# Backward of a gated MLP and a long convolution: transforms with channels as the moving operand, one hand-placed buffer, and transposes moved into DMA

## Chip, cores, metric

One NeuronCore of a Trainium2 chip. The time is the device time of one launch in microseconds (us), the median of several launches. Some launches fall into a slower state, with a lower granted TensorE clock; all runs quoted are in the fast state, and the granted clock of their profiled launches is 0.95 to 0.99.

## The reference

Forward and backward of one block; S = 2048 positions, D = 512 channels, F = 1376, all in bfloat16. Cut to what matters:

```python
def _A_ref(q, k, v, shift_k, ssm_k, ssm_D):         # long convolution by FFT over 2*S points
    k_shift = sum_t k_pad[:, t:t+S, :] * shift_k[:, 3-t]
    kv = k_shift * v
    y = irfft(rfft(kv, 2*S) * rfft(ssm_k, 2*S))[:S] + kv * ssm_D
    return q * y
def _B_ref(x, w_gate, w_up, w_down):                # gated MLP
    return ((x @ w_gate) * (x @ w_up)) @ w_down
xn  = layernorm(A_q)
out = A_q + _A_ref(xn, ...) + _B_ref(xn, ...)
# outputs: out, and the gradients of A_q, A_k, A_v, shift_k, ssm_k, ssm_D, w_gate, w_up, w_down
```

The gradients need three forward transforms (of the filter, of `kv`, of `xn*grad_out`) and three inverse ones, all as matmuls with sine tables, and the MLP's intermediates (`h`, `dg`, `du`) in two layouts: with F on the partitions for the down projections, with positions on the partitions for the weight gradients.

## The kernel before, in the parts that matter

Three stages: the MLP by chunks of 256 positions, whose intermediates go to DRAM as `HDD`; then the transforms, by blocks of 128 channels, interleaved with the down projections (`YB`); then the weight gradients with the finish.

```python
def f_B(key):                                  # second step of a forward transform: 64 matmuls of 128 columns a call, 768 in all
    ...
    for k0 in range(0, 16, 4):
        pb = psF.tile([128, 4, 2, 128], F32, name="pb", tag="psf")
        for ki in range(4):
            nc.tensor.matmul(pb[:, ki, 0, :], lhsT=E[:, k1, 0, :], rhs=Ar, start=True, stop=False)
            nc.tensor.matmul(pb[:, ki, 0, :], lhsT=E[:, k1, 2, :], rhs=Ai, start=False, stop=True)
            ...                                # two more for the imaginary part
        evac_act(Xh[:, 2 * k0: 2 * (k0 + 4), :], pb[:]...)
def i_B(ikey):                                 # inverse transform: the same, then a transposing DMA from SBUF to SBUF
    ...
    nc.sync.dma_start_transpose(out=Ct[:]..., in_=C_sb[:]...)
def nat_from(hb, fw, nat_ap):                  # weight gradients: HDD blocks transposed on TensorE, evicted by ACT
    pt = psF.tile([128, NJ, 128], BF, name="ptw", tag="psf")
    for j in range(NJ):
        nc.tensor.transpose(pt[:, j, :fw], hb[:fw, j * 128:(j + 1) * 128], ident[:fw, :fw])
    evac_act(nat_ap, pt[:, :, :fw])
```

## Time and profile before

| | before |
|---|---|
| time, median (range, n) | 706.23 us (702.38 to 709.43, 15) |
| first stage: MLP and preparation | 0 to 190 us |
| second stage: transforms, down projections | 190 to 480 us |
| hole: TensorE waits for the first `HDD` read | 480 to 496 us |
| third stage: weight gradients, finish | 496 to 707 us |
| TensorE, VectorE, ScalarE busy | 84%, 55%, 56% |

The stages were cut where the first and last instructions of a tile name stand (`pgu`, `pdx`, `ptw`). The prediction below shows the lines. Read a row of the stretches as: length, then the busy time of each engine with its count, then granted clock, share of the DMA engines' time and their rate. An engine is the bound of a stretch only if its busy time nearly fills the length.

### The profile page before, as it was taken

What the parts mean: (1) busy time and instruction counts of PE and PEld (TensorE: products, weight loads), DVE (VectorE), ACT (ScalarE), POOL (GpSimd) and SP (SyncE); (2) the same over time, 40 slices, a digit from 0 to 9 for tenths busy, and PEclk for the clock granted to TensorE, in tenths of its full rate; (3) what the DMA queues carried; (4) which work ended last, traced back from release to release, by engine and by line L of the source; (5) the groups of instructions that cost most, each with busy time, mean ns of one, the idle gap of its engine ahead of it and who ended that gap; (6) DMA issues with size and microseconds to landing.
All of it is one profiled execution on the core that took longest, in us unless ns stands there. A gap on an engine that the chain in (4) does not pass through costs nothing.

```text
span 706.9 us, 12877 instructions
## 1 busy us (share of the span) xinstructions
PE 591.1 (84%) x5194; PEld 407.2 (58%) x5252; DVE 389.5 (55%) x1016; ACT 395.1 (56%) x563; POOL 8.9 (1%) x21
## 2 busy tenths in 40 slices
PE   0889999999779989988889999871998698797992
PEld 0677877888555656665567665441554454463551
DVE  5898965673431536545555456220585608773652
ACT  2669976865573656653467643230665565374542
POOL 3001000000000000000000000000000000000000
PEclk9999999999899999999999999985999799998997
DMA  8648589754395586966968577779999998998433
GB/s 261 215 160 287 198 239 287 272 198 174 143 349 160 166 228 145 229 153 134 260 132 226 123 214 173 169 168 302 329 296 268 273 253 284 299 298 248 130 125 104
DMA packets 205947, 153.28 MB, mean 217 GB/s; under 512 B 120832, under 2 KB 194624, under 8 KB 203840
## 3 DMA queue, kind: packets, MB, share of 16 engines
q1 hardware_dynamic: 202752, 148.10, 73.7%
q10 hardware_dynamic: 3136, 4.36, 1.9%
q8 instruction: 41, 0.67, 0.4%
q14 instruction: 18, 0.15, 0.1%
HBM read 82.68 MB, written 57.19 MB: 198 GB/s over the span
## 4 chain that ended last, share of the span: by engine, by line
PE 40%; DMA 31%; DVE 10%; ACT 10%; issue 4%; SPq 2%; POOL 0%; POOLq 0%; ACTq 0%; DVEq 0%
DMA Ct<-C_sb 13%; PE pg L730 6%; DMA hb<-HDD 3%; PE pgu L472 3%; DMA nat_in<-in_A_k_dram 3%; PE pgu L474 3%; PE pdh L476 3%; DMA bd_j<-BD 3%; ACT C_sb L574 3%; PE pyc L249 2%; PE pb L551 2%; PE ptw L681 2%; PE pdx L557 2%; DMA BD<-bd 2%; PE pdx L556 2%
## 5 line engine op out<-in xcount | busy, mean ns | idle before, releaser
L730 PE MATMUL pg<-nat,xn_tm 128*128 128x512 bf16 (+1 forms) x374 | 80.1, 366 | 0.8 <-issue 0.2
L574 ACT COPY nat<-ptw 128x2048 bf16<-128x2048 bf16 (+1 forms) x33 | 59.1, 1833 | 31.0 <-PE ptw L681 30.9
L574 ACT CAST Xh<-pb 128x1024 bf16<-128x1024 f32 x48 | 47.2, 1013 | 51.3 <-PE pb L617 50.2
L478 ACT CAST gud<-pgu 128x512 bf16<-128x512 f32 (+1 forms) x88 | 51.9, 590 | 32.7 <-ACT gud L479 16.8
L557 PE MATMUL pdx<-WuT_sb,hd_y 128*128 128x512 bf16 (+1 forms) x173 | 66.1, 382 | 0.4
L556 PE MATMUL pdx<-WgT_sb,hd_y 128*128 128x512 bf16 (+1 forms) x164 | 62.7, 382 | 0.1
L681 PE MATMUL ptw<-ident,hb 128*128 128x128 bf16 (+1 forms) x528 | 40.0, 238 | 26.3 <-DMA hb<-HDD 20.6
L472 PE MATMUL pgu<-xnT_all,Wg_sb 128*128 128x256 bf16 (+1 forms) x352 | 56.0, 278 | 4.3 <-ACT gud L478 4.2
L730 PEld LDWEIGHTS <-xn_tm 128*128 128x128 bf16 x384 | 37.7, 101 | 35.4 <-issue 4.0
L476 PE MATMUL pdh<-goT_all,WdT_sb 128*128 128x256 bf16 (+1 forms) x352 | 55.3, 276 | 0.0
L574 ACT CAST C_sb<-pb 128x512 bf16<-128x512 f32 x96 | 49.8, 591 | 9.4 <-PE pb L644 7.8
L681 PEld LDWEIGHTS <-hb 128*128 128x128 bf16 (+1 forms) x528 | 36.1, 108 | 32.2 <-issue 23.4
L474 PE MATMUL pgu<-xnT_all,Wu_sb 128*128 128x256 bf16 (+1 forms) x352 | 54.6, 276 | 0.0
L574 ACT CAST A_sb<-pa 128x1024 bf16<-128x1024 f32 x48 | 45.4, 1044 | 0.2 <-PE pa L600 0.2
L614 PE MATMUL pb<-A_sb,E 128*128 128x128 bf16 x192 | 42.0, 219 | 4.0 <-ACT A_sb L574 2.5
L797 DVE SCALAR_TENSOR_TENSOR acc<-dks,kvk 128x512 bf16<-128x512 bf16 x64 | 43.8, 685 | 0.6
L551 PE MATMUL pb<-Wd_sb,hd_y 128*128 128x512 bf16 (+1 forms) x159 | 43.7, 379 | 0.4 <-issue 0.2
L641 PE MATMUL pb<-Yh,ET 128*128 128x128 bf16 x192 | 41.9, 218 | 1.7 <-ACT C_sb L574 1.0
L480 DVE TENSOR_TENSOR hdd<-gud 128x256 bf16<-128x256 bf16 (+1 forms) x88 | 25.2, 286 | 31.9 <-ACT gud L478 24.6
L617 PE MATMUL pb<-A_sb,E 128*128 128x128 bf16 x192 | 42.0, 219 | 0.0
L644 PE MATMUL pb<-Yh,ET 128*128 128x128 bf16 x192 | 42.0, 219 | 0.0
L616 PE MATMUL pb<-A_sb,E 128*128 128x128 bf16 x192 | 42.0, 219 | 0.0
(171 smaller groups left out, 1245.2 us busy)
## 6 DMA issues: line engine op xcount, KB each, us to landing
HDD<-hdd SPq DMA_DIRECT2D x8, 2112.0 KB, 8.8
hd_y<-HDD SPq DMA_DIRECT2D x8, 2112.0 KB, 9.8
hb<-HDD SPq DMA_DIRECT2D x30, 512.0 KB, 6.7
BD<-bd SPq DMA_DIRECT2D x16, 512.0 KB, 4.0
bd_j<-BD SPq DMA_DIRECT2D x8, 1024.0 KB, 8.6
CTS<-kv SPq DMA_DIRECT2D x4, 1024.0 KB, 5.1
FS<-kd SPq DMA_DIRECT2D x8, 512.0 KB, 5.4
x_cm<-FS SPq DMA_DIRECT2D x8, 512.0 KB, 5.2
```

The costliest lines, as they stand in the source:

```text
L472: nc.tensor.matmul(pgu[:fw, 0, :], lhsT=Wg_sb[:, c, f0:f0 + fw], rhs=xnT_all[:, c, css], start=(c == 0), stop=(c == NCB - 1))
L474: nc.tensor.matmul(pgu[:fw, 1, :], lhsT=Wu_sb[:, c, f0:f0 + fw], rhs=xnT_all[:, c, css], start=(c == 0), stop=(c == NCB - 1))
L476: nc.tensor.matmul(pdh[:fw, :], lhsT=WdT_sb[:, c, f0:f0 + fw], rhs=goT_all[:, c, css], start=(c == 0), stop=(c == NCB - 1))
L478: nc.scalar.copy(gud[:fw, 0:2, :], pgu[:fw])
L551: nc.tensor.matmul(pb[:], lhsT=hd[:fw, 0, fb, ss], rhs=Wd_sb[:fw, fb, :], start=False, stop=(fb == NFB - 1))
L556: nc.tensor.matmul(pdx[:], lhsT=hd[:fw, 1, fb, ss], rhs=WgT_sb[:fw, fb, :], start=(fb == 0), stop=False)
L557: nc.tensor.matmul(pdx[:], lhsT=hd[:fw, 2, fb, ss], rhs=WuT_sb[:fw, fb, :], start=False, stop=(fb == NFB - 1))
L574: nc.scalar.copy(o, i)
L614: nc.tensor.matmul(pb[:, ki, 0, :], lhsT=E[:, k1, 0, :], rhs=Ar, start=True, stop=False)
L681: nc.tensor.transpose(pt[:, j, :fw], hb[:fw, j * 128:(j + 1) * 128], ident[:fw, :fw])
L730: nc.tensor.matmul(pw[:, :R], lhsT=xn_tm[:, j, rows(c)], rhs=nat[:, j, :R], start=(j == 0), stop=(j == NJ - 1))
L797: nc.vector.scalar_tensor_tensor(acc6[:], dks[:, 0:QS], 1.0, kT6[:, 3 - j:3 - j + QS], op0=ALU.mult, op1=ALU.mult, accum_out=dp[:, j:j + 1])
```

## The change

It is a rewrite of the same three stages, meant to make TensorE's work wider and the transfers larger. The sequence is cut as s = 16p + r, so that plain loads and stores are mostly rows of 2 KB and more; the transforms mix over the partitions, with all 512 channels as the moving operand; their intermediates go through DRAM (`AX`, `CX`). Half-array matmuls (64 columns or 64 rows of weights) stand in pairs. The transposes of `HDD` leave TensorE for transposing DMAs. Everything in SBUF lies in one hand-placed buffer, so all its tiles have the name `big` in the profile. The diff cut to its core:

```diff
-    pb = psF.tile([128, 4, 2, 128], F32, name="pb", tag="psf")     # 1536 matmuls of 128 columns in all
-        nc.tensor.matmul(pb[:, ki, 0, :], lhsT=E[:, k1, 0, :], rhs=Ar, ...)
+    def s_B(i, t):                                                 # 192 of 512 columns on 128x64 of the array
+        px = psF.tile([128, 2, D], F32, name="pX", tag="psf")
+        for cp in range(2):
+            for j in range(2):
+                MM(px[64 * j:64 * j + 64, cp, :], lhsT=E[:, 2 * i + j, cp, :], rhs=a[:, j, t, :], start=True, stop=True)
+        ACOPY(X[:, t, :, :], px[:])
+    def s_Bi(i, pr):                                               # 192 of 512 columns on 64x128 of the array
+        for c in range(2):
+            for j in range(2):
+                q = slice(64 * j, 64 * j + 64)
+                MM(pc[:, j, :], lhsT=ET[q, i, c, :], rhs=Y[q, c, :], start=(c == 0), stop=(c == 1))
+        ACOPY(C[:, :, pr, :], pc[:])
-    nc.sync.dma_start_transpose(out=Ct[:]..., in_=C_sb[:]...)      # 12 of 1 MB, SBUF to SBUF
-    nc.tensor.transpose(pt[:, j, :fw], hb[:fw, ...], ident[...])   # 528 on TensorE
+    ldT(out=dst[:, ch, 0:nf, :]..., in_=HDD[ch, :, t, fb0:fb0 + nf, :]...)   # 72 transposing DMAs from DRAM
...
+    while not SG.done:          # second stage: one transform group, then five matmuls of the down projections
+        SG(1)
+        Y(5)
+    while not (WG.done and CG.done):   # third stage: twelve gradient matmuls, then one step of the finish
+        WG(12)
+        CG(1)
```

## The prediction

> **What bounds the kernel now.** I read the page's totals first, then the busy time by stretch, cut at the first and last start of the tiles `pgu`, `pdx`, `ptw`, then the chain, then the forms.
>
> ```profile
> PE 591.1 (84%) x5194; PEld 407.2 (58%) x5252; DVE 389.5 (55%) x1016; ACT 395.1 (56%) x563; POOL 8.9 (1%) x21
> DMA packets 205947, 153.28 MB, mean 217 GB/s; under 512 B 120832, under 2 KB 194624, under 8 KB 203840
> ...
> PE 40%; DMA 31%; DVE 10%; ACT 10%; issue 4%; SPq 2%; POOL 0%; POOLq 0%; ACTq 0%; DVEq 0%
> ```
>
> ```profile
> 28.00:55.00 27.00, 24.05 (x266) 20.14 (x264) 24.09 (x89) 19.61 (x37) 2.58 (x2) 1.00 0.48 151
> 55.00:190.00 135.00, 128.13 (x1163) 107.56 (x1165) 89.83 (x292) 98.54 (x183) 0.10 (x1) 0.97 0.67 228
> 190.00:480.00 290.00, 255.66 (x2434) 169.23 (x2467) 136.22 (x197) 154.81 (x216) 0.00 (x0) 0.98 0.76 191
> 480.00:496.00 16.00, 3.24 (x31) 3.15 (x32) 0.00 (x0) 1.34 (x1) 0.00 (x0) 0.50 1.11 304
> 496.00:690.00 194.00, 169.26 (x1218) 98.93 (x1235) 116.20 (x349) 108.66 (x113) 0.00 (x0) 0.95 0.87 255
> ```
>
> The columns after the length are PE, PEld, DVE, ACT, POOL busy, then granted clock, DMA share and GB/s. There are three stages: A, the gated MLP and the preparation (to 190 us), bound by PE; B, the transforms and the down projections (190 to 480), PE too, with gaps; a hole of 16 us; C, weight gradients and finish (to 707), where PE is at 87% and DMA at 87% (300 GB/s at a share of 1.00 in 500:550). The chain has only 40% in PE and 31% in DMA, so the loss is in waits between the two.
>
> ```profile
> 100.06 0.60 PE L472 MATMUL pgu<-xnT_all,Wg_sb 128*128 128x256 bf16 x4
> 100.50 0.60 PE L474 MATMUL pgu<-xnT_all,Wu_sb 128*128 128x256 bf16 x4
> 258.40 0.38 PE L556 MATMUL pdx<-WgT_sb,hd_y 128*128 128x512 bf16 x1
> 258.61 0.38 PE L557 MATMUL pdx<-WuT_sb,hd_y 128*128 128x512 bf16 x1
> ```
>
> Start to start, not busy time, is the price of a matmul: four of 256 columns in 0.44 us, 109 ns each; 512 columns 215 ns (216 over longer stretches); 128 columns about 56 ns (16 transposes in 0.89 us).
>
> ```profile
> L622 DVE TENSOR_TENSOR Xh<-Xh,Dbc_bf 128x2048 bf16<-128x2048 bf16 x4 | 4.9, 1225 | 18.9 <-ACT Xh L574 18.8
> L198 DVE TENSOR_TENSOR sm_t<-Xh 128x1024 bf16<-128x1024 bf16 x24 | 16.6, 692 | 32.3 <-ACT Xh L574 30.9
> L821 DVE TENSOR_TENSOR m<-xg_j,y_j 128x512 bf16<-128x512 bf16 x16 | 6.7, 420 | 24.4 <-DMA y_j<-YSC 20.3 <-DMA xg_j<-XN 4.2
> L574 ACT CAST Xh<-pb 128x1024 bf16<-128x1024 f32 x48 | 47.2, 1013 | 51.3 <-PE pb L617 50.2
> L478 ACT CAST gud<-pgu 128x512 bf16<-128x512 f32 x80 | 47.2, 591 | 29.5 <-ACT gud L479 15.5 <-PE pgu L474 5.2 <-DVE hdd L482 4.6
> L649 SPq DMA_TRANSPOSE Ct<-C_sb x12: 4728/5396/8076, 254.8 to 466.6; - x12
> 467.00:473.50 6.50, 2.97 (x14) 1.18 (x12) 0.00 (x0) 0.58 (x1) 0.00 (x0) 0.91 0.94 178
> ```
>
> These are my unit prices: a bf16 product of 2048, 1024, 512 elements takes 1.23, 0.69, 0.42 us (a broadcast operand, as in L622, keeps the rate), an eviction of 1024 or 512 takes 1.01 or 0.59 us. A transposing DMA of 1.05 MB holds the queue 5.4 us and, nearly alone in 467.0 to 473.5, fills the DMA engines at only 178 GB/s.
>
> **What the Trainium skill says.** "TensorE: Matmul & The Clock Gate", section "Wait — 56ns, not 53.3ns?", gives 55.6 and 215.7 ns back to back for 128 and 512 columns; the trace agrees (56 and 215). "TensorEngine Tiling (Array Packing)", section "Key Properties", says that tiles run independently but that a change of tiling mode drains the array; no packed pair runs in this trace, so both are open. "DMA: Bandwidth & Descriptors", section "Latency and other measured facts", gives 261 GB/s for a transposing DMA with a non-contiguous middle dimension; the trace shows 178 for one from SBUF, and none from DRAM. The same page, "Rules for kernel authors", asks for large transfers and contiguous last dimensions; here 120832 of 205947 packets are under 512 B.
>
> **The change part by part.** It is a rewrite with the same three stages, on one hand-placed buffer. The sequence is cut as s = 16p + r, so that loads and stores are rows of 2 KB and more; transforms mix over partitions with time outside and channels as the 512-wide moving operand; intermediates AX and CX go through DRAM.
>
> Matmul columns by the built program (both kernels counted): before about 1.31 million, after 1.165 million; matmuls 5252 to about 3085. At the prices above, by stage:
>
> A. Gate, up and down gradient: 1056 x 109 ns = 115 us, unchanged. First transform 96 x 216 = 21, transposes (128 + 64) x 56 = 11. Together 147 us against about 155 of PE busy there before. ACT: 96 evictions of 512 (88 gate/up, 48 mostly 512 wide for the gradient, so about 136) x 0.59 = 79 us, 48 x 1.01 = 49, sine tables 15: 143. DVE: 48 x (0.42 + 0.69) = 53, 80 products or copies of 1024 = 55, eight copies of 2048 = 10, layer norm 20, tables 15: 153. Bytes: loads 13 MB, AX 12.6, HDD 17.3, KS 2.1, weights 4: about 48 MB, 150 us at 320 GB/s. Four resources are level, so none hides the waits of another. The first MLP chunk started at 24.8 us before; I leave it at 24, since weights and two groups of x come first in both. Then chunk 0 at 14, chunks 1 to 6 at 121, chunk 7 at 14, and 12 for stalls: A ends at 185, 5 earlier than now.
>
> B. Down projections 528 x 216 = 114 us, unchanged (16 identity matmuls go). Transforms: 192 + 192 matmuls of 512 columns, 83 us if one at a time, in place of 1536 x 56 + 192 x 109 + 64 x 216 + 128 x about 50 = 127 us. They use half of the array (64 columns, or 64 rows), in pairs; if each pair overlaps it is 42. I take 50 for them and 15 for draining: 180, and 10 for stalls. ACT: 96 x 1.01 + 32 x 0.59 = 116. DVE per round 2 x 1.23 + 2 x 0.69 + 6 x 0.42 = 6.4, sixteen rounds 102. DMA 38 MB, 115 us. So PE bounds B at 190, with 5 for the change of stage: 195 against 290. The twelve transposing DMAs, 13% of the chain, leave it.
>
> C. PE: weight gradients 176 x 216 + 256 x 216 + 128 x 163 (384 columns) = 114; last transform 64 x 216 + 128 x 56 = 21; shift gradient 64 x 216 = 14: 149. The 528 transposes (30 us of PE), the 64 four-tap matmuls and the 33 evictions of 1.83 us go. DVE per chunk of 256 rows: 17 us (20 products of 1024 at 0.69, six accumulating 512s at 0.7 to 0.77, small ones), 139 in all. DMA: CX 12.6 MB, loads 11.5, outputs 14.7, so 39 MB plain at 300 to 340 GB/s, 115 to 130 us; and 17.3 MB of HDD read by 72 transposing DMAs: 97 us at 178 GB/s, 66 at the page's 261. Sum 181 to 227, more than PE. I take 205 for C, and 8 for the last stores, against 227 now (with its hole). The gain of larger rows is largely spent on transposing in the DMA.
>
> Sum: 185 + 195 + 205 + 8 = 593; I say 595 us, 16% less.
>
> **The rivals.** First, transposing from DRAM is much slower than from SBUF, or holds the in-order SP queue, in which the stores of the finish wait for DVE and the next loads stand behind them. At twice the cost C becomes about 300 and the whole 690: no gain. For it: 178 GB/s and 5.4 us of queue per MB even from SBUF. Against it: the page's 261. Second, the pairs overlap and drain cheaply, and the DMA transposes run at 261: B 165, C 180, whole 545. Third, pairs do not overlap and each of 96 groups drains the array twice: B 225 to 230, whole 630. Fourth, A stalls because ACT, in order, waits for AX stores behind HDD stores of 2.1 MB (8.8 us to landing now): 15 to 20 us more.
>
> **Range and chances.** The middle of B is 165 to 225, of C 180 to 240; errors partly cancel, so 550 to 645. To reach 692 the first rival must hold nearly in full. Faster by over 2%: 0.95; within 2%: 0.03; slower: 0.02.
>
> **What would show it.** In the profile after: A ending at 185 with DVE, ACT and PE each above 75%; the last `po`/`px` at about 380, with PE above 90% in B; starts inside a pair of `pX` or `pC` a few ns apart (overlap) or 216 ns apart (none); in C a DMA share near 1 with PE near 75%, and waits of `pw` for HDD transposes. Rates of those transposes in bytes per busy time settle the first rival. The prediction is wrong if C takes over 240 or under 175, if PE waits in B for ACT or DVE, or if the first stage ends after 200.

## The result

| | before | after |
|---|---|---|
| time, median (range, n) | 706.23 us (702.38 to 709.43, 15) | 585.54 us (584.74 to 589.37, 11) |
| first stage, and what was predicted for it | 190 | 180 (185) |
| second stage | 290 | 178 (195) |
| hole and third stage | 227 | 226 (213) |

The ratio is 0.8302, 95% interval 0.8281 to 0.8323. A ratio here is the mean time of one kernel's fast runs over that of the other's of the same rounds, so it is not quite the ratio of the medians quoted. For experiments the ratio is to the kernel before on the same chip; to set one beside the changed kernel I divide by 0.8302. Differences in us are between medians of different chips (the kernel before has medians of 706 to 710 there), so they can be some 3 us off: x2_plain below is 26 us faster by medians and 29 by ratios.

The page of the changed kernel: totals, packets, chain of waits by engine.

```profile
PE 487.1 (83%) x3043; PEld 255.1 (44%) x3085; DVE 360.3 (62%) x707; ACT 327.4 (56%) x405; POOL 7.7 (1%) x20
DMA packets 123486, 146.85 MB, mean 252 GB/s; under 512 B 89719, under 2 KB 95671, under 8 KB 121526
...
PE 51%; DMA 17%; DVE 16%; ACT 5%; SPq 4%; issue 4%; another core or an unknown queue 0%; ACTq 0%; DVEq 0%
```

TensorE lost 104 us of busy time, and its share of the span stayed; that alone does not show that all of it was on the path (the 30 us of transposes that left the third stage gained nothing there). The bytes are nearly the same, in 60% of the packets, and by the packet records 67,584 of these, of 256 bytes, belong to the new transposes. Now the busy time by stretch, cut at the first MLP chunk, the first `po`, the last `px`, and the last gradient matmul:

```profile
0.00:23.70 23.70, 3.52 (x32) 3.34 (x33) 14.34 (x63) 6.58 (x9) 4.00 (x16) 1.00 0.96 298
23.70:179.90 156.20, 148.27 (x1307) 123.47 (x1320) 126.49 (x233) 126.08 (x192) 2.76 (x3) 1.00 0.79 273
179.90:357.70 177.80, 174.00 (x898) 57.22 (x915) 91.45 (x166) 112.70 (x129) 0.95 (x1) 1.00 0.73 249
357.70:411.00 53.30, 45.82 (x228) 20.09 (x231) 25.71 (x53) 21.77 (x21) 0.00 (x0) 0.97 0.90 243
411.00:545.00 134.00, 108.17 (x553) 48.48 (x556) 75.98 (x146) 51.42 (x50) 0.00 (x0) 0.99 1.01 244
545.00:583.40 38.40, 7.29 (x35) 2.49 (x35) 26.29 (x49) 8.89 (x7) 0.00 (x0) 0.61 0.51 190
```

The second stage is now TensorE almost without gaps (174 of 177.8), and it gave 112 of the 121 us, though part of that is transform work that the change moved into the other two stages (counted below). The third stage gained nothing: from 411 to 545 the DMA engines are full at 244 GB/s, and then comes a tail of 38 us in which TensorE works 7 us and VectorE 26. The chain agrees that the bound has moved: TensorE from 40% to 51%, DMA from 31% to 17%, DVE from 10% to 16%.

The timeline of the second stage (start, length, engine, line, operation, count):

```profile
250.22 0.61 PE L508 MATMUL pC<-big 64*128 64x512 bf16 x4
...
251.95 0.62 PE L477 MATMUL pX<-big 128*64 128x512 bf16 x4
252.50 1.04 PE L442 MATMUL po<-big 128*128 128x512 bf16 x4
```

A group of four half-array matmuls starts at 251.95, and the next full-array one at 252.50: 0.55 us. The single records show two starts 4 ns apart, the next two 236 ns later, and about 310 ns where 216 is usual on either side of the group. So a group costs 0.55 + 0.095 = 0.645 us, and each change between whole and halved array about 0.1.

### The profile page after: what moved, and what is told of

Same layout as the page of the kernel before. It is cut to its first block, busy times and chain, and to the rows that moved or that the text cites.

```text
span 583.4 us, 8223 instructions
## 1 busy us (share of the span) xinstructions
PE 487.1 (83%) x3043; PEld 255.1 (44%) x3085; DVE 360.3 (62%) x707; ACT 327.4 (56%) x405; POOL 7.7 (1%) x20
## 4 chain that ended last, share of the span: by engine, by line
PE 51%; DMA 17%; DVE 16%; ACT 5%; SPq 4%; issue 4%; another core or an unknown queue 0%; ACTq 0%; DVEq 0%
PE pg L353 7%; PE px L450 6%; PE px L448 6%; PE po L442 6%; DMA big<-HDD 5%; PE pw L717 5%; PE pw L704 5%; PE pX L477 4%; PE pC L508 4%; DMA big<-CX 4%; PE pd L360 3%; SPq L690 3%; DMA big<-in_A_shift_k_dram 3%; DVE big L381 2%; DVE big L365 2%
## 5 line engine op out<-in xcount | busy, mean ns | idle before, releaser
L717 PE MATMUL pw<-big 128*128 128x512 bf16 (+1 forms) x384 | 86.4, 365 | 20.2 <-DMA big<-HDD 19.8
L353 PE MATMUL pg<-big 128*128 128x256 bf16 (+1 forms) x704 | 88.2, 273 | 0.4
L353 PEld LDWEIGHTS <-big 128*128 128x128 bf16 (+1 forms) x704 | 69.6, 100 | 12.9
L450 PE MATMUL px<-big 128*128 128x512 bf16 (+1 forms) x172 | 65.4, 380 | 0.9 <-issue 0.8
L448 PE MATMUL px<-big 128*128 128x512 bf16 (+1 forms) x169 | 64.3, 381 | 0.5 <-issue 0.5
L478 ACT CAST big<-pX 128x1024 bf16<-128x1024 f32 x48 | 48.4, 1014 | 25.4 <-PE pX L477 18.1
L509 ACT CAST big<-pC 128x1024 bf16<-128x1024 f32 x48 | 48.6, 1012 | 23.4 <-PE pC L508 20.8
L354 ACT CAST big<-pg 128x512 bf16<-128x512 f32 (+1 forms) x88 | 52.2, 605 | 14.2 <-PE pg L353 13.1
L401 ACT CAST big<-pa 128x1024 bf16<-128x1024 f32 x48 | 48.7, 1035 | 9.1 <-remote 3.9
L360 PE MATMUL pd<-big 128*128 128x256 bf16 (+1 forms) x352 | 47.2, 273 | 1.0 <-ACT big L354 0.7
L442 PE MATMUL po<-big 128*128 128x512 bf16 (+1 forms) x169 | 44.1, 381 | 0.8 <-issue 0.6
L704 PE MATMUL pw<-big 128*128 128x512 bf16 (+1 forms) x172 | 41.2, 389 | 0.4 <-issue 0.3
L721 ACT CAST big<-pw 128x512 bf16<-128x512 f32 (+1 forms) x24 | 13.6, 584 | 44.4 <-DMA out_dram<-big 24.5
L360 PEld LDWEIGHTS <-big 128*128 128x128 bf16 (+1 forms) x352 | 34.8, 100 | 8.2 <-issue 0.9
```

The lines of the kernel that those rows point to most:

```text
L353: MM(pg[:fw, j, :], lhsT=W[:, c, fb * 128:fb * 128 + fw], rhs=T[:, 0, c, :], start=(c == 0), stop=(c == 3))
L354: ACOPY(g[:fw, 0:2, i, :], pg[:fw])
L360: MM(pd[:fw, i, :], lhsT=WdT[:, c, fb * 128:fb * 128 + fw], rhs=T[:, 1, c, :], start=(c == 0), stop=(c == 3))
L401: ACOPY(a[:, :, t, :], pa[:])
L442: MM(po[:], lhsT=h[:fw, 0, fb, ss], rhs=wy["d"][:fw, fb, :], start=(fb == 0), stop=(fb == NFB - 1))
L448: MM(px[:], lhsT=h[:fw, 1, fb, ss], rhs=wy["g"][:fw, fb, :], start=(fb == 0), stop=False)
```

## The experiments

Line numbers of experiments can be a few off those of the changed kernel. Twelve kernels ran; each is correct unless said otherwise.

**x1_unpack: break the pairs by order.** Both uses of one half come first, then both of the other.

```diff
-        for cp in range(2):
-            for j in range(2):
+        for j in range(2):
+            for cp in range(2):        # in s_B; the same swap of c and j in s_Bi
```

> The changed kernel with the two inner loops of the transforms' matmuls swapped, so that of each group of four only the middle two neighbours use different halves of the array; same matmuls, same results. Theory 1 (stage B is bound by PE and the overlap of the pairs is what made it 178 us): each of the 96 groups grows from two steps of 216 ns to three, B by 21 us (to 199), the whole from 585 to 606; 41 us if no neighbours overlap at all. Rival (B is bound by evictions, products or transfers, and the overlap is worth nothing): the whole within 4 us of 585.

Measured: 586.89 us (585.25 to 589.32), ratio 0.8284: no change. That looks as if pairing did not matter, but it doesn't show it. The order is swapped in the built program too, yet the single records still come in pairs 6 to 7 ns apart, and in 43 of the 47 complete `pC` groups the second record carries the semaphore update that only the third matmul of the program has. So, by the records, TensorE started the third, on the free half, ahead of the second, which had to wait for its own half. One `pC` group did run in the program's order, with its third weights loaded late; it shows what the others avoided, 0.78 us to the next start in place of 0.55 (that group, then a usual one):

```profile
201.77 0.85 PE L508 MATMUL pC<-big 64*128 64x512 bf16 x4
202.55 0.62 PE L477 MATMUL pX<-big 128*64 128x512 bf16 x4
```

```profile
250.78 0.61 PE L508 MATMUL pC<-big 64*128 64x512 bf16 x4
251.33 0.39 PE L442 MATMUL po<-big 128*128 128x512 bf16 x1
```

The experiment did not take away what it was to take away; x7_half does.

**x7_half: no pairs at all.** Both matmuls of each pair use the same half.

```diff
-                MM(px[64 * j:64 * j + 64, cp, :], lhsT=E[:, 2 * i + j, cp, :], ...)
+                MM(px[0:64, cp, :], lhsT=E[:, 2 * i + j, cp, :], ...)
-        ACOPY(X[:, t, :, :], px[:])
+        ACOPY(X[0:64, t, :, :], px[0:64])      # the other half of X is set to zero once
-                q = slice(64 * j, 64 * j + 64)
+                q = slice(0, 64)
```

> Swapping the order inside the groups changed nothing (first batch), so this run denies the pairing altogether: all four matmuls of a group go to the same half of the array (the first 64 columns, or the first 64 rows); number, columns and mode changes stay. The result is wrong on purpose (out2 to out5 and what hangs on them). Theory 1 (two matmuls in different halves run side by side, whatever their order in the queue): a group becomes 4 x 216 ns + 0.2 us of change = about 1.05 us in place of 0.645, so 96 groups cost 40 us more; the second stage goes from 178 to about 215 us and the whole to 620 to 630 us. Rival (a matmul on half of the array simply takes half the time by itself): no change, 584 to 590 us.

Measured: 626.37 us (623.08 to 628.25), ratio 0.8827, out2 to out6 wrong. Its timeline and its second stage:

```profile
252.14 1.05 PE L479 MATMUL pX<-big 128*64 128x512 bf16 x4
253.12 1.25 PE L442 MATMUL po<-big 128*128 128x512 bf16 x5
```

```profile
180.00:396.00 216.00, 214.44 (x901) 74.85 (x900) 90.86 (x164) 112.80 (x127) 6.12 (x3) 1.00 0.60 204
```

From group to next start it is now 0.98 us in place of 0.55, so 96 groups cost 96 x 0.43 = 41 us more; the stage went from 178 to 216 (the first gradient matmul starts at 398.5 in place of 358.0). That shows the pairs to overlap and to be worth 38 to 41 us. The rival is refuted: a half-array matmul alone takes as long as a whole one.

**x2_plain: what the transposing reads cost.** The 72 DMAs read the same bytes plainly; out7 to out9 wrong.

```diff
-            ldT(out=dst[:, ch, 0:nf, :].rearrange("p f (r q) -> p (f r) q", r=2), in_=HDD[...]...)
+            ld(dst[:, ch, 0:nf, :].rearrange("p f s -> p (f s)"), HDD[...]...)
```

> The changed kernel with the 72 transposing reads of HDD made plain reads of the same bytes into the same places; three weight gradients are wrong on purpose. Theory 2 (stage C is bound by the DMA engines, and transposing costs them far more than the same bytes plain): 17.3 MB fall from about 97 us of the engines to about 54, C from 226 to 190 to 200 us, the whole to 550 to 560. Rival (C is bound by DVE and PE chains and by the in-order queue; transposing is hidden): the whole stays within 6 us of 585.

Measured: 559.38 us (557.01 to 560.85), ratio 0.789: 26 us less than the changed kernel. The issues of these reads in the SP queue, with minimum, median and maximum in ns, in the changed kernel and then in this one:

```profile
L690 SPq DMA_TRANSPOSE big<-HDD  x72: 1229/1276/4311, 331.3 to 534.4; - x72
```

```profile
L690 SPq DMA_DIRECT2D big<-HDD  x72: 319/382/677, 332.8 to 496.2; - x72
```

The stretches of the third stage in this run:

```profile
357.70:411.00 53.30, 47.69 (x239) 20.83 (x237) 25.72 (x53) 21.58 (x21) 0.00 (x0) 0.97 0.87 292
411.00:520.00 109.00, 102.39 (x560) 48.92 (x559) 74.23 (x145) 51.27 (x50) 0.00 (x0) 0.98 0.88 304
520.00:555.20 35.20, 6.48 (x36) 2.34 (x34) 26.95 (x49) 8.89 (x7) 0.00 (x0) 0.60 0.33 122
```

Transposing, the DMA engines are full at 244 GB/s; plain, they move 304 at a share of 0.88, and TensorE (102 of 109) becomes the bound. By the packet records, those of 256 bytes in the changed kernel less those left in this run, the transposes' 17.3 MB took 103 us of all 16 DMA engines (168 GB/s), and the same bytes plain some 53. The queue too is held longer, and longer than its median tells: the 72 issues add up to 123 us in place of 26, and from 411 to 545 the SP queue is issuing for 119 of the 134 us. This run relieves engines and queue at once, so it does not tell them apart; x6_actst below does in part. The tail of 35 us is still there: it is not made by the transposes.

**b1_plain: the same question of the kernel before.** Its twelve `Ct` transposes, 13% of its chain, made plain; results wrong.

```diff
-        nc.sync.dma_start_transpose(out=Ct[:]..., in_=C_sb[:]...)
+        nc.sync.dma_start(Ct[:]..., C_sb[:]...)
```

> The kernel before with its 12 transposing transfers of C_sb made plain transfers of the same bytes; results wrong on purpose. If the transposing transfers on the chain (13% of it, 95 us) are what B lost before and what the rewrite took away, the kernel falls from 706 to 620 to 650. If they only filled time in which PE had other work, and the loss was the 243 us of matmul steps, it falls by less than 20 us, to 690 or so. I expect the second, about 695.

Measured: 695.6 us (693.96 to 696.83), ratio 0.9814 (0.9763 to 0.9865): 13 us of 710.1 on that chip, as expected (about 695); by the 2% bar the verdict is unclear, but the interval lies wholly below 1. 13% of the chain would be 92 us. TensorE's waits for `Ct` in the second stage were only 21.5 us to begin with (13.9 + 7.6) and fell to 8.0 (6.3 + 1.7), 13.5 less; the rest of the 92 us lay beside TensorE's other work. A share of the chain is not what its removal saves. (Here the bytes still travel; the change drops these transfers and sends `CX` through DRAM instead.)

**x3_o5: the costliest eviction.** ACT writes out5 as single bfloat16 values 32 bytes apart; swapping two loops writes pairs.

```diff
-            o5v = o5[:].rearrange("p q (j r) -> p q r j", r=R)
-            ACOPY(o5v[:, :, r0:r0 + 2, :], p5[:])
+            o5v = o5[:].rearrange("p q (j r) -> p q j r", r=R)
+            ACOPY(o5v[:, :, :, r0:r0 + 2], p5[:].rearrange("p q r j -> p q j r"))
```

> The changed kernel with the eviction of p5 walking the two neighbouring rows innermost, so that its writes are runs of two elements instead of single ones 32 bytes apart; same results. If the 4.57 us of that eviction are a cost per separate write, it falls to about 2.3 us; if a cost per element of a strided walk, it stays at 4.6. If it is on stage C's critical path, the kernel gains 8 x 2.3 = 18 us; if ACT has room, under 4 us. I expect 2.3 us and a gain of 3 us.

Measured: 588.27 us (587.35 to 589.72), ratio 0.8303: no gain. The eviction itself, before the edit (changed kernel) and with it (minimum, median, maximum in ns):

```profile
L615 ACT CAST big<-p x8: 4513/4576/4627, 371.3 to 550.7; 128x1024 bf16<-128x1024 f32 x8
```

```profile
L615 ACT CAST big<-p x8: 1077/1100/1143, 378.3 to 554.6; 128x1024 bf16<-128x1024 f32 x8
```

4.58 us fell to 1.10, more than expected, nearly as fast as a contiguous one (1.01). The Trainium skill, "SBUF — State Buffer", section "Door 1: The DMA port swizzle (why `[64,N]` ≈ `[32,N]`)", says in a note that SBUF is reached in lines of 16 bytes and that two or more hits in a line are needed for full rate; the trace agrees: one value per line is slow, two are not. The 28 us saved on ACT gave no time, since ACT was 52 us of 134 busy there.

**x4_start: the first 24 us.** The small loads leave the ACT queue, and four DVE copies that wait for them go behind the second layer norm.

```diff
-    nc.scalar.dma_start(skl[:], ...)
-    nc.scalar.dma_start(Drow[:], ...)
     vload(0)
+    ld(skl[:], ...)
+    ld(Drow[:], ...)
-        (in tab_small) for j in range(4): VCOPY(SK[:, j, :], skl[:, :, j])
+    (after ln(1)) sk_copy()
```

> The small loads of D and of the shift kernel leave the ACT queue for the SP queue behind the first loads of x, and the four DVE copies of the shift kernel go behind the second layer norm; the result stays right. Theory (the first 24 us are set by ACT and DVE standing in order behind these small loads: waits of 12.8 and 20.4 us): the first gate matmul starts at 14 to 17 us in place of 23.7, and the whole falls by 6 to 10 us. Rival (the weights of the gate, 2.8 MB, are what it waits for): the start moves by less than 3 us and the whole by less than 3.

Measured: 589.41 us (588.3 to 591.91), ratio 0.8322: no gain. The first gate matmul did move from 23.7 to 20.1 us. Twenty microseconds later it was lost (the changed kernel, then this one):

```profile
40.00:60.00 20.00, 17.76 (x161) 14.63 (x162) 14.94 (x30) 13.83 (x22) 0.00 (x0) 1.00 0.64 233
```

```profile
40.00:60.00 20.00, 14.74 (x118) 11.75 (x116) 15.40 (x34) 11.37 (x17) 0.00 (x0) 0.88 0.65 255
```

TensorE waited there for DVE's products (4.6 us in one wait). The timeline of DVE shows why: the four copies now stand at 47.7 us, and the shift products that need them start at 49.0, where they started at 41.2 in the changed kernel, then behind their own load. So the edit took one wait away and put another in its place, and the first stage ended 2 us later than without it. Neither theory foresaw that; whether an order without both waits would keep the 3.6 us is open.

**x6_actst: stores of the gradients from the other queue.**

```diff
-                    st(out_9[f0:f0 + fw, :], o[:fw])
+                    nc.scalar.dma_start(out_9[f0:f0 + fw, :], o[:fw])      # the same for out7 and out8
```

> The 35 stores of the three weight gradients are issued from the ACT queue and no longer stand in the SP queue among loads and transposes; result stays right. Theory (in-order SP queue: the stores stand behind transposing reads, and ACT waited 24.5 us for their buffers): 5 to 10 us less. Rival (the DMA engines are full in this stage, 0.99 to 1.01 busy, so the queue is not what is short): less than 3 us.

Measured: 587.54 us (586.43 to 588.65), ratio 0.8284: the rival's result. ACT's wait of 24.5 us for output buffers is gone from its list of waits, and its time is spent waiting for TensorE instead (47.6 us). From 411 to 545 the SP queue issues for 105 us in place of 119, the DMA engines stay full (share 1.03), and nothing is gained: that speaks for the engines as the limit, though the transposes themselves still stand in the queue.

**x5_order: the interleaving.**

```diff
-        WG(12)
+        WG(9)
```

> In the last stage nine in place of twelve weight gradient matmuls are issued per step of the finish; result stays right. Theory (the last 38 us, where PE is busy 7 us, are the finish of the last rows, left over because the weight gradients are issued too early): the finish ends sooner and the whole falls by 8 to 20 us. Rival (the last stage is bound by bytes and by the transposing reads, which are then only issued later): within 3 us, the tail shrinks but the gradients end later.

Measured: 578.02 us (577.06 to 579.26), ratio 0.8151, that is 1.8% less than the changed kernel, at the lower end of the expectation.

```profile
411.00:545.00 134.00, 107.89 (x519) 45.73 (x517) 81.77 (x164) 55.36 (x49) 0.00 (x0) 0.93 0.99 259
545.00:562.00 17.00, 16.54 (x88) 8.01 (x86) 10.79 (x18) 4.37 (x8) 0.00 (x0) 0.94 1.02 247
562.00:576.00 14.00, 0.00 (x0) 0.00 (x0) 5.98 (x11) 0.03 (x1) 0.00 (x0) 0.57 0.30 100
```

The tail fell from 38 to 14 us, but the gradients end 17 us later: the DMA engines are full all the way to 562. Both theories hold in part: 8 us (10 by the ratio) came from the order, and the full DMA engines are the likely reason that the rest did not; no run tests that apart.

**c1: x5_order, x3_o5 and x6_actst together.**

> Three edits together: nine gradient matmuls per step, the paired eviction of out5 (1.10 in place of 4.57 us on ACT), and the gradient stores from the ACT queue. In the run with nine per step the chain went through the slow eviction and through ACT's wait for stores. Theory (each of the two edits that gave nothing alone was hidden behind the tail and pays now): 568 to 574 us. Rival (bytes and transposing reads bound the stage): 576 to 580, as with nine alone.

Measured: 575.96 us (575.27 to 579.45), ratio 0.8153: the same as x5_order. The two edits that gave nothing alone gave nothing behind it either; the DMA share was 1.02 from 411 to 520.

**x8_peT: undo the move of the transposes.** `HDD` is read plainly and its 128 x 128 blocks are transposed in place on TensorE, evicted by ACT.

```diff
-            ldT(out=dst[...], in_=HDD[...])
+            ld(dst[:, ch, 0:nf, :]..., HDD[...])
+    def nat_turn(n, k):                         # four times per group of gradients
+        pt = psF.tile([128, 2, nf, CH], BF, name="ptn", tag="psf")
+        (for each of its blocks) nc.tensor.transpose(pt[...], dst[...], ident[:])
+        ACOPY(dst[:, 2 * k:2 * k + 2, 0:nf, :], pt[:])
```

> One part of the change is undone: the 528 blocks of 128 x 128 of the gradients' operand are loaded plainly and transposed on TensorE again, in place (36 groups of up to 16 through PSUM, each evicted by ACT), in place of 72 transposing DMAs; all else as in the changed kernel, result stays right. Theory (the last stage is bound by the DMA engines, and the transposing reads cost some 26 us of it, as the wrong run with plain reads showed; TensorE has 55 us free there for 30 us of transposes, ACT 140 us free for 36 x 1.85 = 67): 560 to 575 us. Rival (moving them to the DMA queues was right: TensorE and ACT, in order, lose in new waits what the DMA gains): 583 to 610 us.

Measured: 588.09 us (584.58 to 591.27), ratio 0.8304: the rival's time. Its stretches:

```profile
520.00:545.00 25.00, 24.95 (x168) 13.26 (x168) 12.05 (x25) 13.00 (x14) 0.00 (x0) 0.95 0.39 121
545.00:560.00 15.00, 11.81 (x66) 5.80 (x66) 10.04 (x16) 8.07 (x9) 0.00 (x0) 0.89 0.16 55
560.00:588.00 28.00, 3.89 (x12) 0.75 (x11) 20.13 (x40) 5.97 (x4) 0.00 (x0) 0.56 0.35 132
```

The DMA engines were relieved (0.39 from 520 on), but with the same WG(12) the finish of the last rows came behind 30 us more of TensorE's work: the tail (28 us) stood, and the gradients ended at 556 in place of 545.

**c2: x8_peT, with an order that fits it** (each transposing group counts as four of the twelve matmuls; x3_o5 and x6_actst as well).

> Transposes on TensorE as in the run named x8_peT, paired eviction and stores from ACT, and each transposing group counts as four matmuls in the interleaving, so that the finish and the gradients end together. Theory (the last stage is then level: DMA about 190 us, TensorE 180): 550 to 562 us. Rival (ACT or TensorE order costs as much as the DMA gains): 575 to 590 us.

Measured: 559.37 us (557.12 to 561.42), ratio 0.7908, 4.7% below the changed kernel.

```profile
411.00:520.00 109.00, 103.27 (x763) 57.48 (x767) 73.67 (x147) 66.59 (x64) 0.00 (x0) 0.98 0.87 293
520.00:545.00 25.00, 24.95 (x174) 13.71 (x173) 16.78 (x32) 13.23 (x15) 0.00 (x0) 1.00 0.41 153
545.00:560.00 15.00, 4.01 (x28) 2.28 (x25) 8.27 (x15) 1.39 (x3) 0.00 (x0) 0.77 0.17 53
```

TensorE is now the bound, and the DMA engines are little used at the end (0.41, then 0.17). x8_peT alone gave 0, the three order and eviction edits of c1 gave 10, and together with the fitting order they give 26. My reading is that two limits stood in series (full DMA engines, leftover finish), and lifting one left the other. A rival is not excluded: c2 also has the paired eviction and the stores from ACT, which may pay only beside transposes on TensorE, and x8_peT with the mended order alone was not run.

**d1: the last three of nine gradient groups back on transposing DMAs**, WG(11), two buffers for the accumulator of the shift gradient.

```diff
+    def pe_side(n): return n < 6               # groups 6 to 8 by ldT, the others by nat_turn
-        f["dk"] = m.tile("fdk", [128, 2, D])
+        f["dk"] = [m.tile(f"fdk{i}", [128, 2, D]) for i in range(2)]
-        WG(12)
+        WG(11)
```

> The best of the study, mended where its profile still shows waits: as c2, but the last three of the nine gradient groups (where c2's DMA engines are only 0.37 to 0.68 busy and its TensorE full) go back to transposing DMAs, eleven matmuls per step keep the two interleaved streams level, and the accumulator of the shift gradient has two buffers (DVE waited 32.4 us in c2 for its stores). Result stays right. Theory (c2's last stage is bound by TensorE up to 549 us, then 10 us of finish): 11 us of transposes leave TensorE and the tail shrinks to 5, so 544 to 552 us. Rival (the transposing DMAs delay loads and stores of the finish as before): 556 to 565 us.

Measured: 546.01 us (544.92 to 548.93, 6 runs), ratio 0.7728 (0.7689 to 0.7768), correct: the fastest, 6.9% below the changed kernel (0.7728 / 0.8302).

```profile
411.00:520.00 109.00, 102.16 (x655) 51.89 (x653) 74.87 (x145) 52.97 (x58) 0.00 (x0) 0.97 1.00 289
520.00:547.00 27.00, 21.47 (x129) 10.94 (x127) 19.98 (x39) 7.56 (x12) 0.00 (x0) 0.99 0.52 179
```

TensorE (102 of 109) and DMA (1.00) are level, and the last gradient matmul starts at 541.7, 5 us before the end. How much of the last 13 us each of its three edits gave was not separated (a small tile was also placed elsewhere to make room).

## Why the prediction was right

595 us was predicted and 585.5 measured; the three stages of the working are off by 5, 17 and 13 us, partly against each other, so that the sum is closer than its parts: that closeness is luck.

- *First stage, 185.* It ended at 180. The start (24) is right to 0.3 us; of the 12 us of stalls hardly 7 came. From the first chunk on, PE, DVE and ACT are busy 95%, 81% and 81%, as the text asked for; counted from 0, ACT has 74%, just under the 75% named. The fourth rival (ACT behind stores, 15 to 20 us more) did not come: no store is named among ACT's waits there; the largest, 13.1 us in total, is for TensorE, and 3.9 us are for something that the profile does not name. That x4_start moved its start but not its end fits "Four resources are level": a wait made on DVE at 40 to 60 us reached TensorE at once.
- *Second stage, 195.* It took 178. The 65 us for transforms and draining (50 + 15) measured 96 x 0.645 = 62, and 528 x 0.216 = 114 holds; together 176. The terms that were too large are the 10 us of stalls and the 5 for the change of stage: 2 us in all. The third rival (no overlap, B 225 to 230) is what x7_half made: 216 us.
- *Where the 112 us of that stage came from.* Before: 290 = 114 for projections, 3.5 for sixteen identity matmuls, 125 for transforms at the unit prices (the medians 56, 109 and 216 ns start to start are in the trace; the 128 small ones cost 34, where the text took 50), so some 47 of waiting. After: 114 + 62 + 2. So 63 us are transforms and 45 are waits. Of the 63, 39 are no saving: they are the first and last steps (192 x 109, 64 x 216 and 128 x 34 ns), which the change moved into the first and third stages, at 21 us each by the prediction's count. The middle steps themselves went from 86 us (1536 x 56) to 62, 24 less; x7_half shows that without pairs they would have grown, to about 103. Of the 45 us of waits, b1_plain puts some 13 down to the transposing DMAs. What the others were has not been tested singly.
- *Third stage, 213 with the last stores.* It took 226. The mechanism is right: the DMA share is 1.01 with TensorE at 81%, and x2_plain puts the transposes' cost at 26 us. The DMA engine time of the transposes was to be 97 us and measured 103. Two terms were mis-sized, against each other: the gradients ended 187 us into the stage, not 205, and the 8 us "for the last stores" were too few: the tail is 38 us, and it is mostly VectorE's finish of the last rows (26 of the 38), left over by the interleaving of twelve matmuls to one step. x5_order shows 24 us of it to be order, though only 8 to 10 of them came off the whole.
- *The first rival* (transposing DMA far slower from DRAM) fails on size: 168 GB/s of the engines, near the 178 seen from SBUF, and the stage took 226, not 300. Its other half, the held queue, is real (119 of 134 us), but taking stores off it gained nothing (x6_actst). *The second rival* is right that the pairs overlap, 4 ns apart, but not that they drain cheaply (0.2 us a group, 19 in all, where the prediction took 15), and wrong in 261. Its own terms add up to 538, not 545.
- The text said that the gain of larger rows "is largely spent on transposing in the DMA". Undoing that alone gave nothing (x8_peT); with the order mended it gave 16 us beyond what order and evictions gave (576 to 559, c1 to c2), and d1, which splits the transposes between the two engines, gave more than either, with two other edits in it.

## What to carry to other kernels

Use the halves of the array in pairs where a transform fills only 64 rows or columns: they ran side by side here in both orders of instructions that were tried (but for one group), and each change of mode cost about 0.1 us. A stage limited in two places, such as full DMA engines and a leftover tail, shows no gain when one is lifted; look at the last 40 us of the profile, and try the edits that gave nothing again together before dropping them. Where a piece of work can be done by DMA or by TensorE, try splitting it by stretch: give it to whichever the profile shows idle there, not to one for good. The fastest run here does so, though its gain is not that edit's alone.

## What the Trainium skill lacked or had wrong

- "TensorEngine Tiling (Array Packing)", "Key Properties", says that a change of mode drains the array, but not what it costs. Here: 310 ns from start to start across a change where 216 is usual, so about 0.1 us per change and 0.2 per group.
- The same page has tiles as independent, but doesn't say that a matmul of a free tile starts ahead of an earlier one whose tile is occupied, and "TensorE: Matmul & The Clock Gate", "The mechanism", says the contrary: matmuls start and end in program order, without reordering. By the records of x1_unpack the third matmul of a group started 6 to 7 ns after the first, before the second, in 43 of 47 `pC` groups, and the time did not change (586.9 against 585.5 us).
- "DMA: Bandwidth & Descriptors", "Latency and other measured facts", gives 261 GB/s for transposing DMAs with a non-contiguous middle dimension. Here the DMA engines were full at 244 GB/s of mixed traffic with transposes, where plain traffic moved 304 at a share of 0.88; the packets of the 72 transposes took 103 us of all engines for 17.3 MB, 168 GB/s; whether their middle dimension counts as non-contiguous in the page's sense, no run shows. For transposes of this size I found no page with the time that one holds the issuing queue: for 256 KB or less 1.28 us in the median and 1.71 in the mean, against 0.38 and 0.37 for a plain read of the same bytes.
- "SBUF — State Buffer", the note on 16-byte lines, gives no size for the penalty. Here an ACT eviction of 1024 values per partition took 4.58 us with one value per line and 1.10 with two.
